# A fused attention and mixture-of-experts kernel: all key and value loads of batch 0 issued at the start, and its exponentials taken 512 columns at a time

## The chip, the cores and the metric

The kernel runs on one core of one Trainium2 chip. Five engines work side by side: TensorE (PE, with its weight loads PEld), VectorE (DVE), ScalarE (ACT), GpSimd (POOL), and SyncE (SP), whose sequencer issues nearly all loads and stores here. [...] The metric is the device time of one execution in microseconds.

## The reference, cut to what matters

```python
batch, n_heads, seq, head_dim = (4, 8, 576, 64)      # n_features m = 128
def phi(x):
    proj = np.einsum('bhsd,md->bhsm', x, omega)
    sq = np.sum(x * x, axis=-1, keepdims=True) / 2.0
    h = proj - sq
    h = h - np.max(h, axis=-1, keepdims=True)
    return np.exp(h) / np.sqrt(m)
q_p, k_p = (phi(q_s), phi(k_s))
kv = np.einsum('bhsm,bhsd->bhmd', k_p, v)
z = np.sum(k_p, axis=2)
out = einsum(q_p, kv) / (einsum(q_p, z) + 1e-06)
```

The result goes through an RMS norm, a gated feed-forward layer (2304 tokens, 512 to 1536 to 512), a router that gives each of 8 experts 288 tokens, and the experts' two layers. All data are float32. The change touches only the keys and values of batch 0.

## The kernel before

**Work items.** The attention stage is a list of 88 items, 22 for each of the 4 batches: 12 key items (4 pairs of heads `p`, 3 groups `g` of 256, 256 and 128 positions), then 10 query items. Each loop turn ("tick") starts one item and carries the earlier ones on. A key item is split on ACT and POOL into a high and a low part (L334, L335), projected on PE by three matmuls of 256 columns for each 128 positions (L354 to L356, `proj`), and then `feat` takes the maxima on DVE (L360) and one exponential on ACT for each 128-column piece, with the negated maximum as its bias (L363). One tick later PE multiplies the result with the values (L392, two trace records for each matmul), and at the end of a pair ACT copies the sum out (L402). A full item has 512 columns in four pieces, the last of a pair 256 in two.

**Loads.** `load_k` loads the keys of a pair (`kt`) and its values (`vt`) into a pool with two buffers of each. It is called three ticks ahead from the loop. SP issues in order, so a load whose buffer is still in use holds back everything behind it.

**Weights.** Among the ticks, 24 units of the gate and value weights and 12 of the output weights are converted: a load into one of three staging buffers (L494), a magnitude on ACT (L498), three DVE operations (L502 to L504), then a cast on ACT and a subtraction on POOL into a buffer `wc` (L526, L527). The pool `wpool` has 12 buffers `wc` of 128x2x1024 floats, one for each chunk of feed-forward weights; the ninth to twelfth are filled last. The pace is 0.3 units a tick before tick 23, and about two a tick after it. As soon as 256 tokens have left the attention and a chunk is converted, the feed-forward matmuls (L571 to L573) join in.

**Order.** The order on every engine is fixed when the kernel is built, by a scheduler that goes by program order, priorities (attention work gets a bonus) and a model of when each operand is there.

Before the first tick the program loads the keys and values of pair 0, then the projection matrix `om`, which ACT scales and splits into `omh` and `oml` (L677 to L679), then constants (`cf`, `wg2s`), three weight units, and `gr`.

Of the kernel before, what the change touches and what calls it, by code (L numbers as in the profile page):

```python
# [9 lines left out]
F32 = mybir.dt.float32  # L10
# [3 lines left out]
AF = mybir.ActivationFunctionType  # L14
OP = mybir.AluOpType
# [4 lines left out]
B, H, S, D, M = 4, 8, 576, 64, 128  # L20
# [258 lines left out]
def kernel(ctx, tc, qT, kT, v1, om, wgv, rms, wo, wg2, w1, w2, cfd, trd, cid, out, dbg=None):  # L279
    nc = tc.nc  # L280
    dbg = dbg or {}
    keep = ctx.enter_context(tc.tile_pool(name="keep", bufs=1))
    wpool = ctx.enter_context(tc.tile_pool(name="wpool", bufs=12))
# [28 lines left out]
    kq = ac.enter_context(tc.tile_pool(name="kq", bufs=2))  # L312
# [7 lines left out]
    xblk, ready = {}, []  # L320

    def load_k(b, p):
        kt = kq.tile([128, 640], F32, name="kt")
        nc.sync.dma_start(kt, kT[b, p])
        vt = kq.tile([128, 5, 2, D + 1], F32, name="vt")
        nc.sync.dma_start(vt, v1[b, p])
        kts[b, p], vts[b, p] = kt, vt

# [26 lines left out]
        nc.tensor.matmul(pp, xh, oml, start=False, stop=False)  # L355
        nc.tensor.matmul(pp, xl, omh, start=False, stop=True)  # L356

    def feat(pp, n, ng):
        mx = at.tile([128, 4], F32, name="mx")
        nc.vector.tensor_reduce(out=mx[:n, :ng], in_=pp[:n, :ng], axis=AX.X, op=OP.max, negate=True)  # L360
        ft = at.tile([128, 4, M], F32, name="ft", bufs=3)
        for g in range(ng):
            nc.scalar.activation(ft[:n, g], pp[:n, g], AF.Exp, bias=mx[:n, g:g + 1])  # L363
        return ft

    class KItem:
# [2 lines left out]
            self.ts = [t for t in (2 * g, 2 * g + 1) if t < 5]  # L369

        def load(self):
            if self.g == 0:
                load_k(self.b, self.p)

        def split(self):
# [19 lines left out]
        def el(self, lag):  # L395
            b, p, g = self.b, self.p, self.g
            if lag == 0:
                self.ft = feat(self.pp, 128, 2 * len(self.ts))
            elif lag == 1 and g == 2:
                if p == 0:  # L400
                    kvs[b] = at.tile([128, H, D + 1], F32, name="kvs")
                nc.scalar.copy(kvs[b][:, 2 * p:2 * p + 2, :].rearrange("p h d -> p (h d)"),  # L402
                               st.pop(("pk", b, p))[:, :2 * (D + 1)])

    class QItem:
# [34 lines left out]
        def el(self, lag):  # L440
            n, b, t, hf = self.n, self.b, self.t, self.hf
            if lag == 0:
                self.ft = feat(self.pp, n, 4)
            elif lag == 1:
                self.qp = at.tile([128, 4, 128], F32, name="qp")
# [220 lines left out]
    items = []  # L666
# [3 lines left out]
    useq = [WgvUnit(f, g) for f in range(KF) for g in range(2)] + [WoUnit(f) for f in range(KF)]  # L670
    AHEAD = 3

    items[0].load()
    ws = stage.tile([128, 2 * M], F32, name="ws")
    nc.sync.dma_start(ws, om)
    oms = fp.tile([128, 2 * M], F32, name="th")
    nc.scalar.mul(oms, ws, SCALE)  # L677
    nc.scalar.copy(omh, oms)
    nc.vector.tensor_sub(oml, oms, omh)  # L679
    items[0].split()  # L680
    nc.sync.dma_start(cf, cfd)
    for it in items[1:AHEAD]:
        it.load()
    nc.sync.dma_start(wg2s, wg2)
    for u in useq[:3]:
        u.load()
    nc.sync.dma_start(gr, rms)
    nc.vector.memset(cs, -0.5)

# [357 lines left out]
```

## Time and profile before

| what | value |
|---|---|
| median of 3 runs | 1029.64 us (1024.87 to 1031.0) |
| profiled execution | 1027.82 us, span 1026.0 us |
| PE busy | 987.4 us, 96% of the span |
| DVE, ACT, POOL busy | 543.8, 402.8, 259.0 us |
| chain that ended last | PE 77%, issue 10%, DVE 7%, POOL, ACT and DMA 2% each |

The page gives shares over the whole span. What one stage is limited by is read from windows of that stage. [...]

### The profile page before, as it was taken

Reading aid. Unit: us, or ns where it says so; the run is one execution under the profiler, and the core shown is the slowest. Engines: PE = TensorE matmul, PEld = TensorE weight load, DVE = VectorE, ACT = ScalarE, POOL = GpSimd, SP = SyncE. Lnnn points to the kernel's source line nnn. Section 1 sums busy time; section 2 is a strip of 40 time slices with the busy share of each in tenths; the row PEclk is TensorE's granted clock in tenths of the full one; section 3 lists DMA queues with packets and bytes.
Section 4 is the critical chain, followed back from the end, with each engine's and each line's share of the span. In section 5 each row is a group of like instructions: output and inputs, shape, how many; then the busy total and the mean of one; then the engine's idle time right before and its main releaser. Section 6 shows DMA issues by size and latency. Waiting matters only on the chain.

```text
span 1026.0 us, 19401 instructions
## 1 busy us (share of the span) xinstructions
PE 987.4 (96%) x7689; PEld 904.2 (88%) x7689; DVE 543.8 (53%) x1244; ACT 402.8 (39%) x1011; POOL 259.0 (25%) x342
## 2 busy tenths in 40 slices
PE   6999899999999999999999999999997999999996
PEld 6889889988998999999999877777776999999996
DVE  5769984653563334523225365555555656555531
ACT  6766555654554434422225100100003554454420
POOL 4536652321233222222224100000004212222111
PEclk9869999999999999999999999999998999999999
DMA  7625672365444311622224466566535756556400
GB/s 256 189 68 184 219 253 70 117 205 183 129 144 131 117 52 42 186 109 82 83 83 165 136 182 185 169 201 176 154 115 161 256 188 199 191 194 207 148 24 24
DMA packets 107082, 153.32 MB, mean 149 GB/s; under 512 B 8176, under 2 KB 72304, under 8 KB 106992
## 3 DMA queue, kind: packets, MB, share of 16 engines
q1 hardware_dynamic: 103920, 142.65, 43.0%
q0 software_dynamic: 3072, 9.44, 2.8%
q8 instruction: 60, 0.98, 0.4%
q14 instruction: 30, 0.25, 0.1%
HBM read 111.17 MB, written 40.89 MB: 148 GB/s over the span
## 4 chain that ended last, share of the span: by engine, by line
PE 77%; issue 10%; DVE 7%; POOL 2%; ACT 2%; DMA 2%; SPq 0%; POOLq 0%; DVEq 0%; ACTq 0%
PE py L843 16%; PE gv L571 9%; PE gv L572 9%; PE gv L573 9%; PE pm L433 3%; PE pm L392 2%; PE cnt L162 2%; PE ph L931 2%; PE ph L933 2%; PE ph L932 2%; PE py L941 2%; PE py L942 2%; PE py L943 2%; DVE dw L503 2%; PE pm L429 2%
## 5 line engine op out<-in xcount | busy, mean ns | idle before, releaser
L571 PE MATMUL gv<-xh,wc 128*128 128x256 f32 x864 | 255.3, 296 | 5.5 <-DVE h L585 5.4
L572 PE MATMUL gv<-xl,wc 128*128 128x256 f32 x864 | 252.0, 292 | 0.0
L573 PE MATMUL gv<-xh,wc 128*128 128x256 f32 x864 | 251.1, 291 | 0.0
L843 PE MATMUL py<-wc,ht 128*128 128x512 f32 x648 | 175.9, 409 | 0.0
L571 PEld LDWEIGHTS gv<-xh,wc 128*128 128x128 f32 x864 | 167.3, 194 | 9.5 <-DVE h L585 6.5
L572 PEld LDWEIGHTS gv<-xl,wc 128*128 128x128 f32 x864 | 167.4, 194 | 1.2
L573 PEld LDWEIGHTS gv<-xh,wc 128*128 128x128 f32 x864 | 167.3, 194 | 1.0
L587 POOL TENSOR_TENSOR hp<-h,hp 128x256 fp32r<-128x256 f32 x108 | 88.2, 817 | 206.2 <-ACT hp L586 201.2
L843 PEld LDWEIGHTS py<-wc,ht 128*128 128x128 f32 x648 | 114.4, 188 | 21.9
L584 DVE SCALAR_TENSOR_TENSOR th<-th,gv 128x256 f32<-128x256 f32 x108 | 45.1, 417 | 123.2 <-ACT th L583 123.0
L363 ACT ACTIVATE ft<-pp,mx 128x128 f32<-128x128 f32 (+1 forms) x320 | 93.9, 371 | 32.4 <-DVE mx L360 31.0
L825 DVE TENSOR_TENSOR wc<-ws,wc 128x1024 fp32r<-128x1024 f32 x58 | 70.9, 1224 | 32.4 <-ACT wc L824 31.7
L583 ACT ACTIVATE th<-gv 128x256 f32<-128x256 f32 x108 | 41.5, 384 | 107.6 <-PE gv L573 107.3
L931 PE MATMUL ph<-exh,wc 128*128 128x288 f32 x256 | 79.0, 310 | 0.0
L941 PE MATMUL py<-ehh,wc 128*128 128x288 f32 x256 | 77.8, 304 | 0.0
L933 PE MATMUL ph<-exh,wc 128*128 128x288 f32 x256 | 76.4, 299 | 0.0
L932 PE MATMUL ph<-exl,wc 128*128 128x288 f32 x256 | 76.3, 299 | 0.0
L942 PE MATMUL py<-ehl,wc 128*128 128x288 f32 x256 | 75.9, 297 | 0.0
L943 PE MATMUL py<-ehh,wc 128*128 128x288 f32 x256 | 75.8, 296 | 0.0
L586 ACT CAST hp<-h 128x256 fp32r<-128x256 f32 x108 | 43.9, 407 | 68.4 <-DVE h L585 68.0
L360 DVE TENSOR_REDUCE mx<-pp 128x4 f32<-128x512 f32 (+2 forms) x88 | 55.7, 635 | 27.3 <-PE pp L356 25.4
L852 ACT COPY ws<-py 128x512 f32<-128x512 f32 x18 | 10.6, 586 | 147.1 <-PE py L843 137.2
(188 smaller groups left out, 1918.4 us busy)
## 6 DMA issues: line engine op xcount, KB each, us to landing
ws<-in_w_dram SPq DMA_DIRECT2D x64, 512.0 KB, 3.6
h_dr<-hp SPq DMA_DIRECT2D x54, 512.0 KB, 2.8
ht<-h_dr SPq DMA_DIRECT2D x54, 512.0 KB, 4.4
ws<-in_wgv_dram SPq DMA_DIRECT2D x24, 512.0 KB, 4.3
ws<-in_wo_dram SPq DMA_DIRECT2D x12, 512.0 KB, 4.2
dw<-h_dr SPq DMA_DIRECT2D x24, 256.0 KB, 2.8
vt<-in_v_dram SPq DMA_DIRECT2D x16, 325.0 KB, 3.4
kt<-in_kT_dram SPq DMA_DIRECT2D x16, 320.0 KB, 4.2
```

The lines of the kernel that those rows point to most:

```text
L363: nc.scalar.activation(ft[:n, g], pp[:n, g], AF.Exp, bias=mx[:n, g:g + 1])
L571: nc.tensor.matmul(pg[:, v], w[:, 0, k, v], xh[:, k], start=(k == 0), stop=False)
L572: nc.tensor.matmul(pg[:, v], w[:, 0, k, v], xl[:, k], start=False, stop=False)
L573: nc.tensor.matmul(pg[:, v], w[:, 1, k, v], xh[:, k], start=False, stop=(k == KD - 1))
L587: nc.gpsimd.tensor_sub(hl, h, hh)
L843: nc.tensor.matmul(py, ht[:, i4, a], w[:, l, f % 2], start=(f == 0 and n == 0), stop=(f == KF - 1 and n == 2))
L931: nc.tensor.matmul(ph, w[:, 0, k, m], xh[:, k], start=(k == 0), stop=False)
L932: nc.tensor.matmul(ph, w[:, 0, k, m], xl[:, k], start=False, stop=False)
L933: nc.tensor.matmul(ph, w[:, 1, k, m], xh[:, k], start=False, stop=(k == KD - 1))
L941: nc.tensor.matmul(py, w[:, 0, k], hh[:, k], start=(k == 0), stop=False)
L942: nc.tensor.matmul(py, w[:, 0, k], hl[:, k], start=False, stop=False)
L943: nc.tensor.matmul(py, w[:, 1, k], hh[:, k], start=False, stop=(k == KE - 1))
```

## The change

The keys and values of all four pairs of batch 0 go into four buffers of `wpool` (`kt` in the first half, `vt` in the second) and are loaded before the first tick, mixed with the first weight units; `om` is now the first load, and `cf`, `wg2s` and `gr` come later. `feat` gets a second form for the 12 key items of batch 0: DVE adds the negated maxima to the projection and writes to SBUF, and ACT takes one exponential over all columns in place.

```diff
--- before.py
+++ after.py
@@ -320,9 +320,15 @@
     xblk, ready = {}, []
 
     def load_k(b, p):
-        kt = kq.tile([128, 640], F32, name="kt")
+        if b == 0:
+
+            room = wpool.tile([128, 2, 1024], F32, name="wc")
+            kt = room[:, 0, :640]
+            vt = room[:, 1, :10 * (D + 1)].rearrange("p (t h d) -> p t h d", t=5, h=2)
+        else:
+            kt = kq.tile([128, 640], F32, name="kt")
+            vt = kq.tile([128, 5, 2, D + 1], F32, name="vt")
         nc.sync.dma_start(kt, kT[b, p])
-        vt = kq.tile([128, 5, 2, D + 1], F32, name="vt")
         nc.sync.dma_start(vt, v1[b, p])
         kts[b, p], vts[b, p] = kt, vt
 
@@ -355,10 +361,15 @@
         nc.tensor.matmul(pp, xh, oml, start=False, stop=False)
         nc.tensor.matmul(pp, xl, omh, start=False, stop=True)
 
-    def feat(pp, n, ng):
+    def feat(pp, n, ng, whole=False):
         mx = at.tile([128, 4], F32, name="mx")
         nc.vector.tensor_reduce(out=mx[:n, :ng], in_=pp[:n, :ng], axis=AX.X, op=OP.max, negate=True)
         ft = at.tile([128, 4, M], F32, name="ft", bufs=3)
+        if whole:
+            nc.vector.tensor_tensor(ft[:n, :ng], pp[:n, :ng], mx[:n, :ng].unsqueeze(2).to_broadcast([n, ng, M]),
+                                    op=OP.add)
+            nc.scalar.activation(ft[:n, :ng], ft[:n, :ng], AF.Exp)
+            return ft
         for g in range(ng):
             nc.scalar.activation(ft[:n, g], pp[:n, g], AF.Exp, bias=mx[:n, g:g + 1])
         return ft
@@ -369,7 +380,7 @@
             self.ts = [t for t in (2 * g, 2 * g + 1) if t < 5]
 
         def load(self):
-            if self.g == 0:
+            if self.g == 0 and self.b:
                 load_k(self.b, self.p)
 
         def split(self):
@@ -395,7 +406,7 @@
         def el(self, lag):
             b, p, g = self.b, self.p, self.g
             if lag == 0:
-                self.ft = feat(self.pp, 128, 2 * len(self.ts))
+                self.ft = feat(self.pp, 128, 2 * len(self.ts), whole=b == 0)
             elif lag == 1 and g == 2:
                 if p == 0:
                     kvs[b] = at.tile([128, H, D + 1], F32, name="kvs")
@@ -670,20 +681,22 @@
     useq = [WgvUnit(f, g) for f in range(KF) for g in range(2)] + [WoUnit(f) for f in range(KF)]
     AHEAD = 3
 
-    items[0].load()
     ws = stage.tile([128, 2 * M], F32, name="ws")
     nc.sync.dma_start(ws, om)
+    load_k(0, 0)
     oms = fp.tile([128, 2 * M], F32, name="th")
     nc.scalar.mul(oms, ws, SCALE)
     nc.scalar.copy(omh, oms)
     nc.vector.tensor_sub(oml, oms, omh)
     items[0].split()
+    load_k(0, 1)
+    useq[0].load()
+    load_k(0, 2)
+    useq[1].load()
+    load_k(0, 3)
     nc.sync.dma_start(cf, cfd)
-    for it in items[1:AHEAD]:
-        it.load()
+    useq[2].load()
     nc.sync.dma_start(wg2s, wg2)
-    for u in useq[:3]:
-        u.load()
     nc.sync.dma_start(gr, rms)
     nc.vector.memset(cs, -0.5)
 
```

## Rows read from the trace of the kernel before

**Rows 1.** From the profile's page: the busy time of each engine, and the granted TensorE clock in 40 slices of 25.65 us each (tenths of full speed).

```profile
PE 987.4 (96%) x7689; PEld 904.2 (88%) x7689; DVE 543.8 (53%) x1244; ACT 402.8 (39%) x1011; POOL 259.0 (25%) x342
...
PEclk9869999999999999999999999999998999999999
```

**Rows 2.** The stretches into which the span falls, each with the busy time of the engines (instructions in brackets), the granted clock as a share of 2.4 GHz, the share of the DMA engines and GB/s.

```profile
0.00:38.00 38.00, 28.27 (x152) 26.85 (x153) 21.63 (x38) 26.26 (x76) 20.04 (x25) 0.88 0.75 246
38.00:60.00 22.00, 20.22 (x155) 18.29 (x154) 18.52 (x43) 18.33 (x56) 10.02 (x12) 0.97 0.38 107
60.00:80.00 20.00, 20.00 (x112) 18.67 (x111) 10.12 (x24) 11.09 (x36) 5.86 (x11) 0.59 0.29 88
80.00:148.00 68.00, 60.35 (x464) 58.34 (x464) 64.38 (x97) 39.63 (x104) 44.10 (x38) 0.95 0.63 215
148.00:400.00 252.00, 247.88 (x2007) 233.90 (x2007) 120.14 (x305) 126.27 (x379) 73.61 (x107) 0.99 0.39 129
```

**Rows 3.** The first eight microseconds in order of time: start, duration, engine, line, what it does, and in square brackets how long the engine had been idle and what released it. SPq is the sequencer that issues the loads.

```profile
0.75 0.38 SPq L324 DMA_DIRECT2D kt<-in_kT_dram  x1
...
1.18 0.42 SPq L326 DMA_DIRECT2D vt<-in_v_dram  x1
1.66 0.42 SPq L675 DMA_DIRECT2D ws<-in_om_dram  x1
...
3.07 2.65 SPq L494 DMA_DIRECT2D ws<-in_wgv_dram  x3
3.68 0.71 ACT L334 CAST kh<-kt 128x256 fp32r<-128x256 f32 x2 [1.65 <-DMA kt<-in_kT_dram]
...
4.96 0.42 ACT L677 ACTIVATE th<-ws 128x256 f32<-128x256 f32 x1 [0.56 <-DMA ws<-in_om_dram]
...
5.86 0.79 PE L354 MATMUL pp<-omh,kh 128*128 128x256 f32 x2 [5.86 <-ACT omh L678]
...
7.46 0.68 ACT L498 ACTIVATE dw<-ws 128x512 f32<-128x512 f32 x1 [1.65 <-DMA ws<-in_wgv_dram]
```

**Rows 4.** The same view from 8 to 18 us: the first key items on TensorE, DVE and ACT, and the four exponentials of a later full item.

```profile
8.40 0.41 PE L356 MATMUL pp<-omh,kl 128*128 128x256 f32 x1
...
9.58 0.69 DVE L504 SCALAR_TENSOR_TENSOR dw<-ws,dw 128x512 int32<-128x512 int32 x1
10.19 1.28 DVE L360 TENSOR_REDUCE mx<-pp 128x4 f32<-128x512 f32 x2
...
10.90 2.17 ACT L363 ACTIVATE ft<-pp,mx 128x128 f32<-128x128 f32 x8
...
11.32 1.54 PE L392 MATMUL pm<-vt,ft 128*128 128x65 f32 x6 [2.50 <-ACT ft L363]
...
17.86 1.14 ACT L363 ACTIVATE ft<-pp,mx 128x128 f32<-128x128 f32 x4
```

**Rows 5.** The window from 5 to 38 us by line and shape: count, busy us, mean ns of one, and the idle time before them.

```profile
L360 DVE TENSOR_REDUCE mx<-pp 128x4 f32<-128x512 f32 x9 | 6.1, 689 | 8.2 <-PE pp L356 6.6 <-ACT wc L526 0.8 <-ACT ft L363 0.7
...
L498 ACT ACTIVATE dw<-ws 128x512 f32<-128x512 f32 x7 | 4.8, 679 | 2.0 <-DMA ws<-in_wgv_dram 2.0
...
L526 ACT CAST wc<-dw 128x512 fp32r<-128x512 f32 x5 | 3.1, 626 | 1.9 <-DVE dw L504 1.7
```

**Rows 6.** One line's instructions from 0 to 200 us, with the least, median and largest duration in ns, for three lines on DVE.

```profile
L455 DVE TENSOR_TENSOR x<-pm,dn x20: 405/416/429, 44.3 to 195.2; 128x256 f32<-128x256 f32 x16, 64x256 f32<-64x256 f32 x4
...
L475 DVE TENSOR_TENSOR xl<-pm,xh x8: 394/679/692, 58.8 to 192.1; 128x512 fp32r<-128x512 f32 x6, 128x256 fp32r<-128x256 f32 x2
...
L503 DVE SCALAR_TENSOR_TENSOR dw<-ws,dw x28: 676/1008/1773, 8.6 to 181.6; 128x512 int32<-128x512 int32 x28
```

**Rows 7.** Two-microsecond windows, columns as in rows 2.

```profile
16.00:18.00 2.00, 2.00 (x11) 2.00 (x11) 0.87 (x2) 1.01 (x3) 0.96 (x2) 1.00 0.28 113
...
24.00:26.00 2.00, 2.00 (x16) 1.88 (x16) 2.00 (x6) 1.80 (x7) 1.11 (x2) 1.00 0.91 278
26.00:28.00 2.00, 0.90 (x6) 0.69 (x7) 1.12 (x1) 1.34 (x4) 2.00 (x3) 1.00 0.41 118
28.00:30.00 2.00, 2.00 (x12) 1.73 (x11) 1.32 (x2) 1.20 (x4) 2.00 (x3) 0.65 0.98 292
...
36.00:38.00 2.00, 2.00 (x11) 2.00 (x11) 1.42 (x2) 0.98 (x4) 1.11 (x2) 0.50 0.80 294
```

**Rows 8.** In order of time around 27 us: GpSimd's work and the TensorE instruction that waits for it.

```profile
24.91 1.66 POOL L350 TENSOR_TENSOR ql<-qt,qh 128x512 fp32r<-128x512 f32 x1 [0.89 <-DVE qh L349]
...
26.54 1.86 POOL L335 TENSOR_TENSOR kl<-kt,kh 128x256 fp32r<-128x256 f32 x2
...
27.76 0.38 PE L356 MATMUL pp<-omh,kl 128*128 128x256 f32 x1 [1.10 <-POOL kl L335]
```

**Rows 9.** Two-microsecond windows around 60 and 76 us.

```profile
58.00:60.00 2.00, 1.15 (x7) 1.08 (x7) 2.00 (x5) 1.06 (x3) 2.00 (x3) 0.83 0.13 16
60.00:62.00 2.00, 2.00 (x12) 1.74 (x11) 0.58 (x3) 1.88 (x8) 1.08 (x3) 0.50 0.81 279
...
74.00:76.00 2.00, 2.00 (x11) 2.00 (x11) 0.34 (x1) 1.19 (x4) 0.12 (x1) 0.50 0.55 122
76.00:78.00 2.00, 2.00 (x18) 2.00 (x16) 1.45 (x4) 1.81 (x6) 1.85 (x3) 0.91 0.45 116
```

**Rows 10.** What the load queue (SPq) waited for from 0 to 65 us: line, releaser, us in total, times, longest.

```profile
SPq L326 <- PE pp L356: 6.1, 2, 4.5
```

## The prediction, made before the changed kernel ran

> **What bounds the kernel now.** I read the stages first. From 148 us on TensorE is the bound: 247.9 of 252 us busy [rows 2], and the page's clock row stays at 9 in that part [rows 1]. Nothing that the change touches lies there, so whatever it wins or loses arises before 148 us and is handed on as a shift of all that follows. In the opening TensorE is busy too, but slow or waiting: 28.3 of the first 38 us, none of it before 5.86 [rows 2, 3]; from 60 to 80 us it is busy throughout at a mean clock of 0.59. Only from 80 to 148 is another engine full: DVE, 64.4 of 68 us. [...] The second look is the order of time from 0 to 18 us. The first projection waits for `omh`, which waits for the third load in SP's queue [rows 3]. By 8.81 (8.40 and 0.41) twelve matmuls, two items, are through, but their maxima start at 10.19: DVE executes in order, and three operations of a weight unit, the last at 9.58, stand ahead [rows 4]. That unit waited for its own load until 7.46 [rows 3]. TensorE idles 2.50 us there. The third look, windows of 2 us, shows the clock: 11 matmuls in the window at 16 us, 16 at 24 us; at 26 us TensorE is busy 0.90 of 2.00, and from 28 us on the granted clock falls to 0.50, where it still is at 36 to 38 [rows 7].
>
> **The change part by part.**
>
> *The start.* `om` moves from the third place in SP's queue to the first, 1.66 to 0.75 us, and pair 0's keys from 0.75 to about 1.18. `omh` follows `om` through two ACT operations. Everything else unchanged, the first matmul comes 0.9 us earlier, at about 4.95: bounds 0 (the keys, now behind `om`, become the last operand: they came at 3.68 and would at about 4.1, in time) and -0.91. I take -0.9.
>
> *The first exponentials.* Item 0 needs six matmuls; counted at the spacing of the opening, twelve in 8.81 - 5.86 = 2.95 us, that is about 1.5 us, so its projection is whole at about 6.45. If DVE is free: maximum 0.69 [rows 5], new addition 0.68 (price below), exponential 0.65, and TensorE's second phase starts at about 8.5 instead of 11.32 [rows 4], 2.8 us earlier, the 0.9 included. If the weight unit still stands ahead on DVE, its load now lands later: it is again sixth in the queue, but behind 0.66 MB of pair 1 instead of 0.19 MB of constants, at 246 GB/s [rows 2] 1.9 us more, hence 9.4 us in place of 7.46; unit and item then end near 14.2, 2.9 us later than now. Bounds -2.8 and +2.9. The order on DVE is fixed at build time by when the planner expects the operands; the projection is now about 1 us earlier and the weight load later, and both push the maximum to the front. I take -2.8.
>
> *The exchange per item.* A full item trades four exponentials, 1.14 us together [rows 4], for one over 512 columns. The trace of before has none of that width; the nearest are other 512-column passes on ACT, 0.63 and 0.68 [rows 5], so 0.65: 0.49 us less on ACT, eight times 3.9, and 0.2 us for each of the four half items, 4.7 in all. DVE gains an addition that reads PSUM and writes SBUF; nearest are L475, 0.68 for 512 columns, and L455, 0.42 for 256, and neither varies by much, unlike L503 with two SBUF inputs, 0.68 to 1.77 [rows 6]. So 8 x 0.68 + 4 x 0.42 = 7.1 us more on DVE. In the first 38 us DVE is busy 21.6, so the 7.1 fit, at 28.7 of 38, while ACT drops from 26.3 to 21.6 [rows 2]. For one item the path from maximum to last exponential goes from 0.69 + 1.14 = 1.83 to 2.02 us, and TensorE can't begin on the first piece ahead of the last any more; but the projection's PSUM buffer is free 0.46 us sooner (after 1.37 instead of 1.83), which lets the next projection but one start. On the path all twelve would cost at most +1.9 (12 x 0.19, less for half items); relieved ACT gives at most -4.7. Between these I take 0.
>
> *Loads.* Four key and value loads and their issues leave the loop for the start. SP waited 6.1 us for value buffers with everything behind them in line [rows 10]; that goes. No row shows TensorE waiting for a key, value or query load after the first, so I count 0; its bound is -1.5, below which the casts on ACT would be late next. What these buffers take from `wpool` is free again when the last pair of batch 0 is multiplied, at tick 12, and the ninth weight chunk is not due before the faster pace of tick 23: 0. Without that cover, a weight unit at the head of the staging queue would hold DVE's order for as long as the last pair takes.
>
> *The clock after 28 us.* The fall follows a 1.10 us wait of TensorE for `kl`, which queued on GpSimd behind the split of a query block (1.66 us) [rows 8]. The mean of 0.65 from 28 to 30 us puts the fall at 28.6 [rows 7]; at least 9.4 us at half speed, to 38, cost 4.7 us. With 2.8 us less before it, the query load issued earlier and the key parts split earlier, this meeting is different; it may vanish or come elsewhere. Bounds -4.7 and 0; I take half, -2.4, since no row favours either end.
>
> Sum: -2.8 + 0 + 0 - 2.4 = -5.2 us, from the profiled 1027.82 to 1022.6. The median of the runs is 1.8 above that execution, so the forecast is 1024 in terms of the median.
>
> **The rivals.**
>
> *The gain is lost on DVE.* From 80 to 148 us DVE has 3.6 us of idle time [rows 2]. If the 7.1 us push weight units from the opening into that stage, it ends 7.1 - 5.2 = 1.9 us later: 1031. For it: the units' order is static. Against it: DVE idles 9.9 us from 60 to 80, before tick 23's burst.
>
> *The order on DVE stays.* The change then doesn't do what it says at the start: +2.9 instead of -2.8 with the rest as above is +0.5, 1030.
>
> *The clock's long stretch goes as well.* From about 59.3 to 76.4 TensorE is at 0.50 (worked out from the means 0.83 and 0.91 at the two ends [rows 9]), and 17 us at half speed cost 8.5 us. It begins after a window in which TensorE was busy 1.15 of 2.00. A different meeting of queues there gives 1024 - 8 = 1016. [...] I give it 0.2.
>
> *Slower.* The three-step path leaves TensorE waiting in each key item. If the waits come to about 1.1 us, as in the one before the fall at 28 us [rows 8], the clock doesn't rise at 18 us: the 10 us between 18 and 28 then cost 5 more, no start is won, and the 7.1 us on DVE reach the full stage: 1029.6 + 5 + 7.1 = 1042. For it: at 16 matmuls in 2 us the 14 records of a full item take 1.75 us, less than that path. Against it: at 11 in 2 us they take 2.5, so at half speed TensorE is itself the slowest and has no waits, and two items are under way at a time.
>
> **How the numbers follow.** Forecast 0.43, DVE 0.20, order stays 0.10, clock 0.20, slower 0.07. The clock rival lies beyond 1% for the most part (0.17), the forecast's lower end adds 0.08: faster 0.25. Slower takes most of its rival: 0.06. The rest is 0.69. About 1% is what a measurement of this kernel can tell from no change (the runs of before lie between 1024.87 and 1031.0). The range runs from the clock rival less the runs' spread, 1013, to the DVE rival with it, 1034.
>
> **What would show it.** Right: the first matmul near 5 us, the first L392 near 8.5, L360 ahead of L502 on DVE; the addition at 0.68 and the exponential near 0.65; the end of DVE's full stage, now 148 us, some 5 us earlier; no long fall of the clock at 28 us. Wrong: `L502` ahead of the first maxima, a full DVE from 10 to 38 us with weight units late, or a granted clock of 0.50 in stretches where it was 1.00. The weakest step is the clock: each of its stretches is worth as much as all the rest.

## The result, and the profile after

The changed kernel is slower: over 20 runs of each its median is 1033.8 us (1028.59 to 1042.34) against 1026.71 (1017.24 to 1035.31), a ratio of 1.0089 with a 95% interval of 1.0067 to 1.0111. The forecast was a gain of 5 us; the result is a loss of 7. The profiled execution has a span of 1034.0 us, 8.0 more than before. Line numbers below are the changed kernel's: L360 to L362 are the projections, L366 the maxima, L369 the new addition, L371 the wide exponential, L403 the product with the values, L505 to L515 the weight units.

The stages of the changed kernel, columns as in [rows 2]:

```profile
0.00:38.00 38.00, 25.70 (x120) 24.69 (x121) 21.08 (x38) 16.28 (x36) 14.54 (x22) 0.90 0.66 221
38.00:60.00 22.00, 20.52 (x126) 19.26 (x125) 16.14 (x33) 14.82 (x44) 10.68 (x10) 0.70 0.38 112
60.00:80.00 20.00, 18.34 (x155) 17.01 (x156) 16.13 (x41) 17.09 (x52) 8.28 (x15) 1.00 0.19 60
80.00:148.00 68.00, 58.25 (x456) 56.62 (x454) 63.80 (x92) 39.87 (x104) 46.90 (x40) 0.95 0.67 215
```

In the first 38 us TensorE gets 120 matmuls done instead of 152, although DVE is no busier than before (21.1 against 21.6) and ACT has 10 us less to do [rows 2]. The engines weren't overloaded; they worked less. The second row has the clock at a mean of 0.70, where before it was 0.97; in the third it is the other way round, 1.00 where it was 0.59. The last row looks like the one before [rows 2].

When the loss arises is read from ACT's copy of each finished pair of heads (`kvs`) of batch 0. First the kernel before, then the changed one, in order of time:

```profile
18.87 0.28 ACT L402 COPY kvs<-pm 128x130 f32<-128x130 f32 x1
24.47 0.26 ACT L402 COPY kvs<-pm 128x130 f32<-128x130 f32 x1
29.10 0.27 ACT L402 COPY kvs<-pm 128x130 f32<-128x130 f32 x1 [0.34 <-PE pm L392]
38.05 0.27 ACT L402 COPY kvs<-pm 128x130 f32<-128x130 f32 x1
```

```profile
20.54 0.27 ACT L413 COPY kvs<-pm 128x130 f32<-128x130 f32 x1 [0.42 <-PE pm L403]
27.97 0.27 ACT L413 COPY kvs<-pm 128x130 f32<-128x130 f32 x1 [0.56 <-PE pm L403]
36.53 0.27 ACT L413 COPY kvs<-pm 128x130 f32<-128x130 f32 x1 [0.51 <-PE pm L403]
44.92 0.27 ACT L413 COPY kvs<-pm 128x130 f32<-128x130 f32 x1 [4.22 <-PE pm L403]
```

The first pair is 1.7 us late, the last 6.9. The first feed-forward matmul is then 6.0 us late (69.1 against 63.1) and the last 6.7 (579.4 against 572.7): in this pair of profiles most of the loss is made in batch 0's key items. It isn't handed on as a constant shift, though. The four copies of batch 1 are 6.5, 1.4, 5.9 and 4.3 us late, the last of batch 3 5.2; the two executions spend different stretches at half clock.

The start of the changed kernel in order of time, to be held against [rows 3, 4]:

```profile
3.07 0.43 SPq L505 DMA_DIRECT2D ws<-in_wgv_dram  x1
...
4.25 0.71 ACT L340 CAST kh<-wc 128x256 fp32r<-128x256 f32 x2 [1.01 <-DMA wc<-in_kT_dram]
...
4.87 0.40 ACT L689 CAST omh<-th 128x256 fp32r<-128x256 f32 x1
...
5.32 0.80 PE L360 MATMUL pp<-omh,kh 128*128 128x256 f32 x2 [5.32 <-ACT omh L689]
...
9.74 0.66 ACT L509 ACTIVATE dw<-ws 128x512 f32<-128x512 f32 x1 [4.47 <-DMA ws<-in_wgv_dram]
...
10.43 0.43 DVE L513 TENSOR_SCALAR dw<-dw 128x512 int32<-128x512 int32 x1 [4.69 <-ACT dw L509]
...
10.78 1.28 DVE L366 TENSOR_REDUCE mx<-pp 128x4 f32<-128x512 f32 x2
11.97 1.28 DVE L369 TENSOR_TENSOR ft<-pp,mx 128x512 f32<-128x512 f32 x2
12.69 0.63 ACT L371 ACTIVATE ft<-ft 128x512 f32<-128x512 f32 x1 [1.79 <-DVE ft L369]
12.80 0.55 PE L360 MATMUL pp<-omh,kh 128*128 128x256 f32 x1 [4.50 <-DVE ft L369]
...
13.58 0.52 PE L403 MATMUL pm<-wc,ft 128*128 128x65 f32 x2
```

One weight operation (L513) still stands ahead of the first maxima, and its load, issued at 3.07 behind pair 1's, lands at 9.74: DVE idles until 10.43, although both projections are through at 8.30. Then both items' maxima run, then both additions: the first projection buffer is free only when its addition is done, and TensorE has waited 4.50 us for it. Of these, 2.5 us passed before DVE began the maxima; the kernel before also had a wait of 2.50 us at this place, for the exponentials [rows 4]. The same windows as in [rows 7], from the changed kernel:

```profile
16.00:18.00 2.00, 2.00 (x11) 2.00 (x11) 1.55 (x3) 0.21 (x1) 0.19 (x1) 1.00 0.02 5
...
20.00:22.00 2.00, 1.86 (x9) 1.56 (x9) 1.20 (x3) 1.58 (x5) 2.00 (x3) 1.00 0.96 284
...
24.00:26.00 2.00, 2.00 (x12) 2.00 (x11) 0.51 (x1) 0.00 (x0) 0.00 (x0) 1.00 0.79 298
26.00:28.00 2.00, 1.93 (x12) 1.79 (x11) 0.66 (x2) 0.90 (x3) 0.45 (x1) 1.00 0.03 10
28.00:30.00 2.00, 0.63 (x4) 0.47 (x4) 1.83 (x5) 1.24 (x4) 0.72 (x1) 1.00 0.00 0
30.00:32.00 2.00, 2.00 (x12) 2.00 (x13) 2.00 (x5) 1.29 (x3) 1.58 (x2) 0.65 0.03 8
...
48.00:50.00 2.00, 2.00 (x12) 2.00 (x10) 2.00 (x3) 0.01 (x1) 1.06 (x1) 0.50 0.00 0
50.00:52.00 2.00, 1.70 (x12) 1.40 (x12) 1.75 (x3) 2.00 (x6) 1.32 (x1) 0.73 0.71 170
```

From 16 to 28 us TensorE does 9 to 12 matmuls in 2 us, no more than where the granted clock is 0.50 (12 in the window at 48 us), and the kernel before had reached 16 [rows 7]. No run shows a clock in GHz, as [rows 2] and some of the expectations below name it; what the views show is a share of full speed and a pace. At the slow pace, here as where the share is 0.50, matmuls of 256 columns follow each other at 0.21 us, each with a record of at least 0.41 us; at the full pace they are 0.12 us apart, with records of 0.27 to 0.39. The first short record comes at 27.10 us, where the kernel before had it at 18.36. Right after it TensorE waits again:

```profile
26.74 0.56 PE L362 MATMUL pp<-omh,kl 128*128 128x256 f32 x1
27.10 0.32 PE L361 MATMUL pp<-oml,kh 128*128 128x256 f32 x1
27.26 0.28 PE L362 MATMUL pp<-omh,kl 128*128 128x256 f32 x1
...
27.34 1.29 DVE L366 TENSOR_REDUCE mx<-pp 128x4 f32<-128x512 f32 x2 [2.83 <-PE pp L362]
28.54 1.28 DVE L369 TENSOR_TENSOR ft<-pp,mx 128x512 f32<-128x512 f32 x2
...
29.37 0.35 PE L360 MATMUL pp<-omh,kh 128*128 128x256 f32 x1 [1.44 <-DVE ft L369]
```

DVE takes maximum, maximum, addition, addition once more, TensorE waits 1.44 us for the first addition, and from 30.6 the granted clock is 0.50 and stays there until about 51.

### The profile page after: what moved, and what is told of

It is laid out like the page before. It is cut to its first block, busy times and chain, and to the rows that moved or that the text cites. A ratio compares the mean times of both kernels' runs of the same rounds, so it can differ in the third digit from the quotient of the medians.

```text
span 1034.0 us, 19375 instructions
## 1 busy us (share of the span) xinstructions
PE 987.2 (95%) x7689; PEld 904.4 (87%) x7689; DVE 550.3 (53%) x1256; ACT 398.5 (39%) x983; POOL 259.2 (25%) x342
## 4 chain that ended last, share of the span: by engine, by line
PE 76%; issue 9%; DVE 7%; DMA 3%; ACT 2%; POOL 2%; SPq 0%; POOLq 0%; DVEq 0%; ACTq 0%
PE py L856 15%; PE gv L582 9%; PE gv L583 9%; PE gv L584 9%; PE pm L403 3%; PE pm L444 3%; PE cnt L162 2%; PE py L954 2%; PE ph L944 2%; PE py L955 2%; PE py L956 2%; PE ph L946 2%; PE pp L360 2%; PE ph L945 2%; PE pp L361 2%
## 5 line engine op out<-in xcount | busy, mean ns | idle before, releaser
L374 ACT ACTIVATE ft<-pp,mx 128x128 f32<-128x128 f32 (+1 forms) x280 | 82.7, 374 | 27.4 <-DVE mx L366 26.4
L366 DVE TENSOR_REDUCE mx<-pp 128x4 f32<-128x512 f32 (+2 forms) x88 | 55.6, 635 | 27.2 <-PE pp L362 26.9
```

## The experiments

All ratios are to the kernel before, run beside it on the same chip; each interval is 95%. A run is 12 executions (7 of `dve_load`, 6 of `last_old_pp4`) against 23 to 35 of the kernel before. The planner in these texts is the scheduler that fixes every engine's order when the kernel is built. The first four ask which part of the change does the harm.

**Only the loads (`loads_only`).** The new form of `feat` is switched off:

```diff
-                self.ft = feat(self.pp, 128, 2 * len(self.ts), whole=b == 0)
+                self.ft = feat(self.pp, 128, 2 * len(self.ts), whole=False)
```

> The changed kernel with the old exponentials of 128 columns in batch 0 as well: only the early loads and the new order of the queue are left. Theory A (the first weight load lies behind pair 1 in the queue, DVE's first weight operation stands ahead of the first maxima and waits for it until 9.7 us; all the rest follows): still slower than before, ratio 1.005 to 1.010, first maxima after 10.5 us, TensorE idle about 4 us ahead of its first L403. Theory B (the loss comes from the three-step path on DVE, whose waits hold TensorE at 1.2 GHz): no slower than before, 0.995 to 1.002.

Measured 1.0014 (0.998 to 1.0047). The early loads alone cost nothing that can be measured, and give nothing: theory A, the one nearest to my own second rival, fails here, although the first maxima still come at 10.15. Its `kvs` copies, set against those of the changed kernel, show where the two part:

```profile
19.33 0.27 ACT L413 COPY kvs<-pm 128x130 f32<-128x130 f32 x1 [2.16 <-PE pm L403]
27.86 0.29 ACT L413 COPY kvs<-pm 128x130 f32<-128x130 f32 x1
33.08 0.31 ACT L413 COPY kvs<-pm 128x130 f32<-128x130 f32 x1
40.16 0.27 ACT L413 COPY kvs<-pm 128x130 f32<-128x130 f32 x1
```

Up to the second pair they are alike (27.86 and 27.97), and both have TensorE at the slow pace until 25 to 27 us (the granted clock of `loads_only` has means of 0.59 from 10 to 20 us and 0.73 from 20 to 30). The third and fourth pair are 3.5 and 4.8 us apart: there the changed kernel, after its 1.44 us wait, is at 0.50 until 51, while the granted clock of `loads_only` is 1.00 from 30 to 60.

**Only the new form (`whole_only`).** The kernel before with `whole=b == 0` and its old loads:

> The kernel before with the new form of the exponentials in batch 0, loads as before. Theory A: within 0.3% of before. Theory B: slower, 1.005 to 1.010, with the last kvs copy of batch 0 some 5 to 7 us later than the 38.05 us of before.

Measured 1.0079 (1.0043 to 1.0115): nearly the whole loss. Its last `kvs` copy comes at 46.1 us, 8.1 later than in the kernel before. The profiled execution is one of the quickest of the twelve (1028.82 us), and in it the delay is gone again at the last copy of batch 3 (368.24 against 368.19): this trace shows the delay where it arises, not how it reaches the end. What TensorE waited for from 5 to 50 us, in total, times and longest, first in the kernel before, then here:

```profile
PE pm L392 <- ACT ft L363: 2.7, 2, 2.5
PE pp L356 <- POOL kl L335: 1.1, 1, 1.1
```

```profile
PE pp L354 <- ACT omh L683: 5.9, 1, 5.9
PE pp L354 <- DVE ft L363: 5.3, 3, 3.6
```

The wait for the addition (L363 in that kernel) doesn't exist in the kernel before.

**Weight loads later or earlier (`weights_last`, `weights_early`).** The changed kernel with the three weight loads behind all of batch 0's keys and values and `cf`:

```diff
     load_k(0, 1)
-    useq[0].load()
     load_k(0, 2)
-    useq[1].load()
     load_k(0, 3)
     nc.sync.dma_start(cf, cfd)
+    useq[0].load()
+    useq[1].load()
     useq[2].load()
```

> The changed kernel with the first three weight loads put behind all keys and values of batch 0, so that the planner puts the maxima ahead of the first weight operation on DVE. Theory A: first maxima near 7 us, first L403 near 9 us, TensorE's first full speed some 4 us earlier than in the changed kernel, ratio to before 0.994 to 1.000. Theory B: the maxima come early, but the items behind them are as slow as in the changed kernel: 1.004 to 1.010.

and with each of them one place earlier, the first directly behind pair 0:

> The changed kernel with each weight load one place earlier, the first directly behind pair 0. DVE's order again has the weight unit ahead of the first maxima, but its load should land near 7.5 us as before. Theory A: the first maxima come near 9.5 to 10 us and the ratio is 0.998 to 1.004. Theory B: 1.005 to 1.010.

Measured 1.0039 (1.0003 to 1.0074) and 1.0048 (1.001 to 1.0087). With the loads last the maxima come at 8.4 us, but the `kvs` copies still follow each other at 7.8 to 8.4 us. A better start may win back part (the intervals overlap the change's); the items behind it stay slow, as theory B had it, though both ratios lie between the ranges of the two theories. The profiled execution of `weights_early` was an unusually quick one: its span is 1019.3 us against a median of 1030.69, and in it the short matmul records begin at 15 us. One profile of this kernel tells little about its median.

**The addition, or the wide exponential (`no_add`)?** The changed kernel without the addition; batch 0's maxima are taken but not subtracted:

```diff
-            nc.vector.tensor_tensor(ft[:n, :ng], pp[:n, :ng], mx[:n, :ng].unsqueeze(2).to_broadcast([n, ng, M]),
-                                    op=OP.add)
-            nc.scalar.activation(ft[:n, :ng], ft[:n, :ng], AF.Exp)
+            nc.scalar.activation(ft[:n, :ng], pp[:n, :ng], AF.Exp)
```

> The changed kernel without the addition in batch 0: the maxima are still taken, but not subtracted, and one exponential reads all columns straight from PSUM (the result of batch 0 is another one then). Early loads and ACT's saving stay, DVE has no more to do than before. Theory B (the addition, between the maxima and the exponential, is what costs): the loss is gone, 0.992 to 1.001, waits of TensorE on DVE's ft gone. Rival (the wide exponential itself costs, because the values can't be multiplied before all pieces are done): still 1.005 or more.

Measured 0.9988 (0.996 to 1.0017). The wide exponential is harmless; the addition is what costs. TensorE's waits themselves hardly shrink: from 5 to 50 us it waits 4.5 us for the exponentials that free the buffers, where the changed kernel waits 5.9 for the additions. What differs is the pace behind them: the short matmul records begin at 18.17 us instead of 27.10, and the last `kvs` copy comes at 35.34 instead of 44.92.

**DVE's time, or its place (`dve_load`)?** The kernel before, with an unused maximum over the loaded keys for each key item of batch 0:

```diff
                 self.ft = feat(self.pp, 128, 2 * len(self.ts))
+                if b == 0:
+                    m = 2 * len(self.ts)
+                    sx = at.tile([128, 4], F32, name="sx")
+                    nc.vector.tensor_reduce(out=sx[:, :m], in_=kts[b, p][:, :m * M].rearrange("p (g m) -> p g m", m=M),
+                                            axis=AX.X, op=OP.max)
```

> The kernel before with 7.1 us more work on DVE in batch 0 that nothing waits for: for each key item one more maximum over 512 (256) columns of the loaded keys, whose result is unused. Theory B1 (it is the place of the addition on the path of PSUM's buffers, not DVE's time): within 0.4% of before. Theory B2 (DVE's time is what costs, wherever it stands, since weight units are pushed back): 1.006 to 1.010 like the change.

Measured 1.0078 (1.005 to 1.0107), as much as the change, and against B1 as I had put it: nothing waits for these maxima, and yet they cost. Its profile doesn't show by which way. The first three unused maxima are over at 5.28 us; the first wanted ones come at 11.92 instead of 10.19 because they stand behind a weight unit whose load landed at 9.30 instead of 7.46. The last `kvs` copy is only 1.9 us later than in the kernel before. Nor are weight units pushed back at the end, as B2 has it: the last of the 24 gate and value units is finished on POOL from 135.8 us on, in the kernel before from 138.8.

**Four buffers (`after_pp4`, `before_pp4`, `dve_load_pp4`).** Every other key item of batch 0 is projected into one of the two feed-forward PSUM buffers, which are idle until some 60 us:

```diff
-                self.pp = psA.tile([128, 4, M], F32, name="pp", bufs=2)
+                if b == 0 and (3 * p + g) % 2:
+                    self.pp = psG.tile([128, 4, M], F32, name="gv")
+                else:
+                    self.pp = psA.tile([128, 4, M], F32, name="pp", bufs=2)
```

In the changed kernel, in the kernel before, and in the kernel with the unused maxima:

> The changed kernel with four PSUM buffers in place of two for the projections of batch 0's keys (every other item takes one of the two feed-forward buffers, idle then). Theory B1: TensorE no longer waits for the addition to free a buffer; most of the loss goes, ratio to before at most 1.003, batch 0's last kvs copy before 42 us. Theory B2: 1.006 to 1.010, as the change.

> The kernel before with the same four buffers, as the control for the run with four buffers in the changed kernel. Both theories: 0.994 to 1.002; if it wins clearly, the buffers are a gain of their own and the changed kernel with four buffers is to be set against this run.

> The kernel before with the 7.1 us of unused maxima on DVE and with the four PSUM buffers. Theory C (DVE's time costs by way of the two buffers: whatever stands ahead of a maximum on DVE keeps a projection buffer full and TensorE waiting): as fast as four buffers without that work, 0.994 to 0.999 of before. Theory B2 (DVE's time costs because weight units are pushed back into the stage where DVE is full): slower than four buffers without that work by 0.5% or more, 1.000 to 1.005 of before.

Measured 0.9977 (0.9948 to 1.0005), 0.9948 (0.992 to 0.9977) and 0.9973 (0.9943 to 1.0004). With four buffers the change costs 0.3% and the unused maxima 0.25%, each within its uncertainty, instead of 0.9% and 0.8%. So theory C, that DVE's time is expensive because it keeps one of only two buffers full, fits its range and B2 misses it. In the profile of `after_pp4` no wait of TensorE for the addition is left, and the last `kvs` copy comes at 38.15 us, although its 256-column matmuls, 0.12 us apart at 11.9 us, are 0.21 us apart again from 12.9 us to 20 at least, and its second `kvs` copy follows the first by 7.69 us: a slow pace in part of the opening alone doesn't make the key items that late. (Over its whole length this execution, 1029.88 us, was the slowest of its twelve.)

**Order of loads with four buffers (`loads_pp4`, `last_pp4`, `last_old_pp4`).** The changed kernel with the old exponentials and four buffers; with the addition and the weight loads last; and with the old exponentials and the weight loads last:

> The changed kernel with the old exponentials and four PSUM buffers: 0.993 to 0.999 of before, the same as four buffers alone if the early loads give nothing, 0.990 or less if they do once the buffers no longer bind.

> The changed kernel with four PSUM buffers and the first weight loads behind batch 0's keys and values: first maxima near 8 us instead of 10.5. If the start counts, 0.990 to 0.995 of before; if only the buffers count, 0.995 to 1.000 like four buffers in the changed kernel.

> The same with the old exponentials of 128 columns. If DVE's time still costs with four buffers, faster than the run with the addition by 0.3% or more, 0.988 to 0.994 of before; if not, equal to it.

Measured 0.9943 (0.991 to 0.9976), 0.9949 (0.9922 to 0.9976) and 0.9894 (0.9847 to 0.9942). The last beats both kernels. The last two differ by the addition alone and stand 0.5% apart, more than I expected of four buffers; the intervals overlap a little. Set in pairs that differ by the new form alone, the runs (with the two repeats below, `after_again` and `last_old_pp4_again`) give what it costs:

| buffers, order of loads | new form | old form | cost |
|---|---|---|---|
| two, as before | 1.0079 | 1 | 0.79% |
| two, as changed | 1.0089, again 1.0058 | 1.0014 | 0.75%, 0.44% |
| two, weight loads last | 1.0039 | 0.9968 | 0.71% |
| four, as changed | 0.9977 | 0.9943 | 0.34% |
| four, weight loads last | 0.9949 | 0.9894, again 0.9914 | 0.55%, 0.35% |

About half of the cost goes with the two more buffers, the other half stays. Each cost is uncertain by 0.4 to 0.5%, so the halving is likely rather than shown.

**Waiting, or the clock (`after_again`, `keep_busy`, `keep_busy_before`)?** The changed kernel beside itself with six unneeded matmuls after each key item, which the planner puts where it expects TensorE to idle, and the same in the kernel before:

```diff
+                if b == 0:
+                    spare = psG.tile([128, 4, M], F32, name="gv")
+                    for i in range(6):
+                        nc.tensor.matmul(spare[:, :2, :], omh[:, :128], omh, start=True, stop=True)
```

> The changed kernel once more, as the measure for the three runs beside it and for how TensorE's clock in the opening differs from one execution to the next: 1.006 to 1.011 of before; last kvs copy of batch 0 at 42 to 47 us if the pace is set by the order of instructions, anywhere from 35 us on if the clock's luck sets it.

> The changed kernel with six more matmuls of 256 columns after each key item of batch 0, into a feed-forward buffer that nobody reads; the planner puts them where it expects TensorE to wait. [...] Theory D (the half clock is what costs; the waits only keep it there): the clock reaches 2.4 GHz before 15 us and stays, the last kvs copy comes before 42 us in spite of the added work, and the ratio is 1.000 to 1.006, below the changed kernel beside it. Theory E (the waits cost by themselves, the clock is a bystander): later than 45 us, 1.009 to 1.016.

> The kernel before with the same matmuls, as the control. Theory D: 0.994 to 1.002, since its half-clock stretches up to 38 us shrink as well. Theory E: 1.003 to 1.010.

Measured 1.0058 (1.0026 to 1.0091), 0.9989 (0.9955 to 1.0023) and 0.9962 (0.9926 to 0.9997). The changed kernel repeats its opening almost to the tenth (`kvs` at 20.45, 27.83, 36.45, 44.83), so its slow pace is no accident of one profile. Four windows of 10 us, first the changed kernel, then with the added matmuls:

```profile
10.00:20.00 10.00, 7.29 (x35) 7.32 (x35) 6.85 (x12) 4.55 (x11) 2.57 (x5) 1.00 0.73 260
20.00:30.00 10.00, 8.42 (x42) 7.83 (x42) 6.25 (x13) 4.90 (x13) 3.63 (x5) 1.00 0.56 188
30.00:40.00 10.00, 9.10 (x44) 8.94 (x44) 9.00 (x14) 5.58 (x14) 8.49 (x8) 0.52 0.49 159
40.00:50.00 10.00, 9.18 (x42) 8.58 (x42) 6.88 (x10) 3.58 (x13) 2.87 (x2) 0.50 0.17 54
```

```profile
10.00:20.00 10.00, 8.91 (x71) 8.29 (x71) 8.58 (x15) 5.86 (x14) 5.26 (x6) 1.00 0.73 262
20.00:30.00 10.00, 10.00 (x89) 10.00 (x88) 8.67 (x16) 6.69 (x16) 7.47 (x7) 1.00 0.75 241
30.00:40.00 10.00, 9.96 (x83) 9.35 (x82) 9.85 (x18) 8.02 (x24) 6.46 (x8) 1.00 0.41 118
40.00:50.00 10.00, 8.59 (x72) 7.84 (x70) 8.15 (x18) 7.88 (x26) 4.91 (x6) 1.00 0.49 145
```

Twice as many matmuls in the same time, 60 of the 72 useless ones among them, and the last `kvs` copy at 35.38 us instead of 44.83. With more to do, TensorE is done earlier: theory D. The addition is unchanged in this kernel, DVE has the same to do, and 0.7% are back, so the half clock carries much of the loss. The control sets a limit to this: the useless matmuls win 0.4% in the kernel before as well, and against that control the changed kernel is still 0.3% slower instead of 0.6%, a difference within the uncertainty. One more reservation: the planner lays out all engines anew for each kernel, so the added matmuls aren't the only difference.

**The start alone, and each cure with it (`last_old`, `last_old_busy`, `last_old_pp4_again`).** Old exponentials, two buffers, weight loads last; the same with unneeded matmuls; the same with four buffers, once more:

> The changed kernel with the old exponentials, two PSUM buffers, and the first weight loads behind batch 0's keys and values: first maxima near 8.5 us. If the start's 2 to 3 us are handed on to the end: 0.996 to 0.999 of before and below loads_only's 1.0014; if a later stage takes them back: 1.000 to 1.003.

> The changed kernel with the old exponentials, weight loads behind batch 0's keys and values, two PSUM buffers, and six unneeded matmuls after each key item of batch 0. If the clock carries it: 0.988 to 0.994 of before, below the same order without the matmuls (0.9968). If the buffers give something of their own: 0.995 to 0.999.

> The same order with four buffers and without the unneeded matmuls, once more: 0.987 to 0.993 of before, and 1% or more below the changed kernel's 1.006 to 1.009.

Measured 0.9968 (0.9933 to 1.0003), 0.997 (0.9942 to 0.9998) and 0.9914 (0.9882 to 0.9947). Where TensorE is hardly starved (10.00 of 10 us busy from 10 to 20 us in `last_old`, at the slow pace, with records of at least 0.41 us), useless matmuls give nothing net of the time that they take: 82 matmuls there instead of 48, but the last `kvs` copy at 37.22 us against 36.96. Four buffers give another 0.5 to 0.7%: they are not the same cure. The version with four buffers has now won twice, the second time with 1018.47 us against 1025.76, about 1% below the kernel before, where the changed kernel is 0.6 to 0.9% above it.

## Why the prediction was wrong, point by point

The forecast was 5 us less, the result is 7 us more. The median, 1033.8 us, lies just inside the stated range, whose upper end was 1034; since the way was wrong, that is luck. Of the 12 us between, the exchange per item, put at 0, makes about 8 by `whole_only`, and gains of 2.8 and 2.4 that didn't come make the rest, as far as so rough a sum goes.

*The start.* 0.9 us was forecast and 0.54 came (5.32 against 5.86): ACT put two key pieces (L340), whose load landed at 4.25, between the two steps on `om`. Small, and the right sign.

*The first exponentials.* I took -2.8 us, with +2.9 as the other bound, and the other bound came: L513 stands ahead of the maxima, its load landed at 9.74 (9.4 was estimated), and the first L403 is 2.3 us later than before, at 13.58. This was the second rival, at 0.10. It alone doesn't decide, though: in `loads_only`, with the same loads, the first maxima (10.15) and the first L403 (11.29) are neither earlier nor later than in the kernel before, and so is the time. What the start won was spent on waiting for this load.

*The exchange per item, put at 0: the step that failed.* The sizes were right, as this view of the changed kernel from 5 to 50 us shows (count, busy us, mean ns, idle before):

```profile
L360 PE MATMUL pp<-omh,kh 128*128 128x256 f32 x20 | 8.7, 476 | 12.2 <-DVE ft L369 5.9 <-ACT omh L689 5.3 <-ACT wc L537 0.9
...
L369 DVE TENSOR_TENSOR ft<-pp,mx 128x512 f32<-128x512 f32 x8 | 5.2, 680 | 0.0
L371 ACT ACTIVATE ft<-ft 128x512 f32<-128x512 f32 x8 | 5.0, 630 | 2.7 <-DVE ft L369 2.5
```

680 ns for the addition (0.68 forecast), 630 for the exponential (0.65). What I got wrong is what they do to the buffers. I reckoned that a buffer is free after 0.69 + 0.68 = 1.37 us, sooner than before. But where two items arrive together, as at 10.78 and 27.34 us, DVE takes maximum, maximum, addition, addition: the first buffer is free after 0.69 + 0.69 + 0.68 = 2.06 us and the second after 2.74, and before that TensorE can't start the next pair. The first line has the waits, 5.9 us for L369 (4.50 and 1.44), of which the late weight load made 2.5. I set this term to 0 between +1.9 and -4.7; `whole_only` shows it at +0.79%, some 8 us, outside both bounds. In its profile TensorE's waits after the first matmul come to 7.9 us, 3.8 more than before, and the granted clock is 0.50 from 21.3 to 52.0 us, before from 28.6 to 38.8. That the waits bring the half clock about is argued from this and from `keep_busy`, not shown by itself. ACT's saving was real (12 wide exponentials take 6.7 us), but ACT wasn't what the items waited for.

*Loads: 0.* Right within the noise; `loads_only`, which has the start in it too, gives 1.0014.

*The clock: -2.4.* Wrong in sign: the stretch at 0.50 lasts from 30.6 to 51.1 us instead of 28.6 to 38.8. My last rival had the mechanism, waits in each item that keep TensorE at half speed, and a time of 1042; I gave it 0.07, because at half speed TensorE "is itself the slowest and has no waits". That is what the trace shows from 14 to 27 us, and it was no argument against the rival: no waits at half speed just means a slow pair, 7.4 to 8.6 us, where the kernel before did its second and third in 5.6 and 4.6. That pace was never left for long, since the first stretch at full speed met the next 1.44 us wait.

The rival by which the long stretch at 0.50 from 59.3 us goes (0.20, 1016) came true in its condition and not in its time: the changed kernel is at 1.00 from 60 to 80 us, but it had 20 us at 0.50 before that. And it got fewer matmuls done in the opening, 120 in 38 us instead of 152.

*The shift.* Half right: 6.9 us at the last `kvs` copy of batch 0 arrive as 8.0 in the span, but with 1.4 to 6.7 us between, and in `whole_only`'s profile 8.1 us arrive as 1.0. *DVE full from 80 to 148 us:* still so, 63.8 of 68 us. The first rival's place for the loss was wrong: the delay is 6.5 us at the first `kvs` copy of batch 1 (80.39 us) and 4.3 at its last (144.47), so that stage added none.

What stays open: how the 0.4 to 0.8% divide between TensorE's idle microseconds and its half clock, the 0.3 to 0.5% that the addition seems to cost even with four buffers, and by which way the unused maxima of `dve_load` cost as much as the addition.

## What to carry to other kernels

Moving work from a busy engine to one with idle time was not free here, where that work stood between a PSUM buffer's filling and its release (0.4 to 0.8% with two buffers, 0.3 to 0.6% with four): count how long each buffer is held in the order in which the engine takes the items, two at a time if they come in twos, and count the buffers first. Here a wait of 1.1 us was followed by 10 us at half clock, one of 1.4 us by 20, and two more buffers (0.9948 in `before_pp4`) were worth more than a shorter instruction (0.9988 in `no_add`, the wide exponential without the addition); useless matmuls in the gaps helped too, where TensorE was starved (0.7% in the changed kernel). Judge such a change by many runs: single executions of one kernel differed by more than the effect, those of the changed kernel by 13.75 us.

## What the runs showed of the hardware

The granted clock stayed at 0.50 for some 20 us while TensorE's record was 2.00 busy of 2.00 in most windows (30.6 to 51 us of the changed kernel), and TensorE worked at the slow pace, 0.21 us from one 256-column matmul to the next, from 12.8 to 27 us without a gap over half a microsecond. With unneeded matmuls in its gaps (`keep_busy`) it did 19 matmuls of 256 columns in 2.83 us from 9.37 us on, had them 0.12 us apart from 14 us, and the clock column is 1.00 through 50 (from 60 to 80, busy 20.00 of 20 us, its mean is 0.65). The two falls after 28 us follow waits of 1.10 us (28.6, kernel before) and 1.44 us (30.6, changed kernel); after a wait of 1.08 us in `keep_busy`, at 13.28, the records stay short (0.28 us). Nor was dense work enough to leave the slow pace: in `last_old` TensorE was busy 10.00 of 10 us from 10 to 20 and did 48 matmuls, where `last_old_busy` did 82. What makes the clock fall and rise is not shown by these runs. Where the clock column says 1.00 before its first fall, the opening can still be at the slow pace: only the spacing of the matmuls shows it, 11 in 2 us against 16 and more.
